# Turning a Gram product round and respacing a kernel's start: XCiT attention before a GELU feed-forward part

## The chip, the cores and the metric

The kernel runs on one core of a Trainium2 chip. The metric is the time of one execution in device microseconds (us), as the median of several executions. Where a single number of a profile is quoted, it is from one profiled execution, whose span is about 1.8 us shorter than its time. Engine names in the profile: PE is TensorE's matmuls, PEld its weight loads, DVE is VectorE, ACT is ScalarE, POOL is GpSimd, SP is SyncE; a q behind a name is the issuing of DMAs on that engine.

## The reference, cut to what matters

```python
B, N, C, D = 4, 6080, 256, 2048
qn = q / (np.linalg.norm(q, axis=1, keepdims=True) + 1e-06)   # norms over the N rows
kn = k / (np.linalg.norm(k, axis=1, keepdims=True) + 1e-06)
s = kn.transpose(0, 2, 1) @ qn / tau          # 256 x 256 per batch, summed over N
a = softmax(s)                                # over the last axis (q's columns)
x = v @ a                                     # (B, N, 256)
y = gelu_tanh(x @ w_in) @ w_out               # the feed-forward part, D = 2048
```

The kernel folds `a @ w_in` into one matrix `aw` per batch, so the stream is `hp = vT' @ aw`, a gelu on ScalarE and `yp = g' @ w_out`, in 12 blocks of up to 512 rows per batch.

## The kernel before

Batch 0 cannot start until its whole q and k are there: ten chunks of 128-row slots are loaded, cast to bf16, squared and multiplied into the Gram matrix `G`. Idle matmuls, whose results nobody reads, stand between the chunks to keep TensorE busy and so its clock full.

```python
first_chunks = chunks_of([6, 6, 6, 6, 6, 6, 4, 3, 2, 2], 7)  # slots; the 64 remainder rows ride on chunk 7
TAIL, SHARED = 6, 8
fillers = [0, 0, 5, 5, 5, 5, 3, 2, 1, 0]      # idle matmuls ahead of each chunk, for the clock

def stage_chunk(n):                           # called four chunks ahead
    ...                                       # chunks 8 and 9 share the buffers of 6 and 7
    load_chunk((nc.sync, nc.scalar if n < 1 else nc.sync), st, 0, first_chunks[n])   # (queue of q, of k)

def gram(G, qk, s, rows, first, last):        # G[i, j]: i = k's columns on the partitions
    for ic in range(2):
        nc.tensor.matmul(G[:, ic, :], lhsT=qk[:rows, 1, s, ic * 128 : ic * 128 + 128],
                         rhs=qk[:rows, 0, s, :], ...)

def scaled(G, r):                             # row i of G times 1/|k_i|, a value per partition
    for ic in range(2):
        nc.vector.tensor_scalar(Gs[:, ic, :], G[:, ic, :], r[:, 2 + ic : 3 + ic], inv_tau, ...)

def turned(Gs):                               # four fp32 transposes: T[j, i]
    ...

for n, ch in enumerate(first_chunks):         # batch 0
    nc.vector.tensor_copy(qkb[...], st[...])                  # L242, cast
    nc.scalar.activation(sqb[...], st[...], AF.Square)        # L247 (last two chunks: half on VectorE)
    keep_clock(fillers[n])
    ...                                                       # gram per slot, column sums of squares
    stage_chunk(n + 4)
    if n == n_chunks - 4:                                     # the gate: GpSimd's queue waits for chunk 6
        nc.gpsimd.tensor_copy(gate[:, 0:1], st[0:1, 1, 0, 0:1])
...
# behind the gate, on GpSimd's queue: w_in in four quarters, v of block 1, w_out in two halves,
# the first q and k of batch 1, v of block 2
load_v(1)
for half in range(2):
    nc.gpsimd.dma_start(out=wout_bf[...], in_=wout_v[...])
load_qk(1, 0)
load_v(2)
...
eT[:, jc, :] = exp(T[:, jc, :] * r[:, jc])    # 1/|q_j| as ScalarE's scale per partition
# first block: two of the four column groups of aw are made before it, the others within it
for i in range(NP):
    ...                                       # hp (L536 before, L533 after), gelu
    more_aw(1)                                # one of the four products left
```

v of block 2 and later ones is turned by DMA transposes on the sync queue once it has landed (`vT`).

## Time and profile before

| | before |
|---|---|
| time, median of 4 runs | 758.17 us (757.68 to 758.28) |
| profiled span | 756.4 us |
| first `hp` matmul (the feed-forward stream begins) | 43.19 us |
| span less that: the stream | 713.21 us |
| last piece of batch 0's q and k landed | 35.34 us |
| clock at half | 29.7 to 33.1 us |
| last column sum ends / both exponentials end | 38.24 / 41.32 us |

How to read it: the stream is TensorE alone, with no gap worth naming, so its 713.2 us are a constant of the work. Everything above 713.2 is the start, and the place of the first `hp` matmul is the one number that tells what a change to the start was worth. The timeline puts this matmul at 43.19 and the chain at 43.35; I use the timeline.

### The profile page before, as it was taken

Reading aid. Unit: us, or ns where it says so; the run is one execution under the profiler, and the core shown is the slowest. Engines: PE = TensorE matmul, PEld = TensorE weight load, DVE = VectorE, ACT = ScalarE, POOL = GpSimd, SP = SyncE. Lnnn points to the kernel's source line nnn. Section 1 sums busy time; section 2 is a strip of 40 time slices with the busy share of each in tenths; the row PEclk is TensorE's granted clock in tenths of the full one; section 3 lists DMA queues with packets and bytes.
Section 4 is the critical chain, followed back from the end, with each engine's and each line's share of the span. In section 5 each row is a group of like instructions: output and inputs, shape, how many; then the busy total and the mean of one; then the engine's idle time right before and its main releaser. Section 6 shows DMA issues by size and latency. Waiting matters only on the chain.

```text
span 756.4 us, 12305 instructions
## 1 busy us (share of the span) xinstructions
PE 738.3 (98%) x5248; PEld 504.5 (67%) x5248; DVE 278.2 (37%) x484; ACT 419.8 (56%) x411; POOL 70.7 (9%) x127
## 2 busy tenths in 40 slices
PE   4899999999999999999999999999999999999997
PEld 3556666667666666666666666666767666666666
DVE  4644545454402555553421455454441011011011
ACT  5675555555465555555555555555546655555552
POOL 0321011001021011001031000100101000000000
PEclk9999999999999999999999999999999999999999
DMA  8999957225149778313549375621412633322111
GB/s 364 355 206 168 177 84 155 54 42 83 42 93 215 134 137 132 73 43 64 102 93 220 83 135 96 126 79 47 82 42 79 110 83 72 68 76 52 41 57 56
DMA packets 80599, 83.59 MB, mean 111 GB/s; under 512 B 55456, under 2 KB 60064, under 8 KB 80544
## 3 DMA queue, kind: packets, MB, share of 16 engines
q0 software_dynamic: 17648, 32.97, 26.5%
q1 hardware_dynamic: 62672, 48.98, 24.3%
q8 instruction: 41, 0.67, 0.4%
q10 hardware_dynamic: 224, 0.85, 0.3%
q14 instruction: 14, 0.11, 0.1%
HBM read 78.91 MB, written 24.90 MB: 137 GB/s over the span
## 4 chain that ended last, share of the span: by engine, by line
PE 95%; DMA 3%; ACT 1%; DVE 0%; SPq 0%; issue 0%; DVEq 0%; ACTq 0%
PE yp L463 44%; PE hp L536 43%; PE G L141 5%; DMA st<-in_k_dram 3%; PE ps L201 2%; PE cols L153 1%; ACT sqb L247 0%; PE idle L137 0%; PE T L179 0%; DVE qkb L242 0%; SPq L80 0%; ACT g L540 0%; PE ps L345 0%; PE vps L333 0%; DVE Gs L171 0%
## 5 line engine op out<-in xcount | busy, mean ns | idle before, releaser
L540 ACT ACTIVATE g<-hp 128x1024 bf16<-128x1024 f32 (+1 forms) x384 | 389.3, 1014 | 308.9 <-PE hp L536 308.9
L463 PE MATMUL yp<-wout_bf,g 128*128 128x256 bf16 x3040 | 393.3, 273 | 0.0
L536 PE MATMUL hp<-vT,aw 128*128 128x512 bf16 (+1 forms) x1536 | 390.5, 377 | 0.2 <-ACT g L540 0.2
L463 PEld LDWEIGHTS <-g 128*128 128x128 bf16 x3040 | 297.5, 98 | 112.9
L536 PEld LDWEIGHTS <-aw 128*128 128x128 bf16 x1536 | 150.0, 98 | 105.3 <-issue 1.1
L480 DVE COPY ysb<-yp 128x512 f32<-128x512 f32 (+1 forms) x95 | 64.9, 683 | 403.1 <-PE yp L463 395.1
L404 DVE TENSOR_TENSOR acc<-acc,sq 128x512 f32<-128x512 f32 (+1 forms) x141 | 97.6, 692 | 4.8
L141 PE MATMUL G<-qkb 128*128 128x256 bf16 (+1 forms) x384 | 70.7, 285 | 13.6 <-DVE qkb L242 13.6
L403 DVE TENSOR_TENSOR sq<-qkb 128x512 bf16<-128x512 bf16 (+1 forms) x141 | 58.9, 418 | 0.0
L141 PEld LDWEIGHTS <-qkb 128*128 128x128 bf16 (+1 forms) x384 | 38.2, 102 | 23.0 <-DVE qkb L242 15.6
L280 POOL DMA_DIRECT2D vb<-in_v_dram x47 | 25.5, 544 | 142.8 <-DMA vT<-vb 135.9
L210 DVE TENSOR_SCALAR aw<-ps,rsinv 128x512 bf16<-128x512 f32 x30 | 22.3, 750 | 25.6 <-PE ps L201 25.3
L80 POOL DMA_DIRECT2D qkb<-in_q_dram x24 | 13.0, 540 | 152.1 <-PE hp L536 83.0
L247 ACT ACTIVATE sqb<-st 128x3072 bf16<-128x3072 f32 (+3 forms) x9 | 20.4, 2286 | 11.2 <-DMA st<-in_k_dram 11.2
L242 DVE CAST qkb<-st 128x3072 bf16<-128x3072 f32 (+4 forms) x11 | 14.7, 1345 | 14.9 <-DMA st<-in_k_dram 14.9
L201 PE MATMUL ps<-win_bf,eT 128*128 128x512 bf16 x60 | 17.7, 379 | 0.0
L414 POOL TENSOR_TENSOR r<-r,half 128x4 f32<-128x4 f32 x3 | 3.1, 1041 | 141.5 <-DVE r L413 141.5
L80 POOL DMA_DIRECT2D qkb<-in_k_dram x24 | 13.1, 544 | 5.0 <-DMA qkb<-in_q_dram 2.2
L521 POOL COPY g<-gr 128x1024 bf16<-128x1024 bf16 x2 | 2.1, 1037 | 104.1 <-PE yp L463 104.1
L439 DVE RECIPROCAL den<-den 128x256 f32<-128x256 f32 x6 | 10.5, 1753 | 0.2
L549 POOL COPY gr<-g 128x1024 bf16<-128x1024 bf16 x2 | 2.1, 1034 | 87.6 <-ACT g L540 87.6
L137 PE MATMUL idle<-filler 128*128 128x512 bf16 x32 | 9.2, 408 | 0.0
(60 smaller groups left out, 81.0 us busy)
## 6 DMA issues: line engine op xcount, KB each, us to landing
out_dram<-ysb SPq DMA_DIRECT2D x44, 512.0 KB, 2.9
vb<-in_v_dram POOLq DMA_DIRECT2D x43, 256.0 KB, 8.5
qkb<-in_q_dram POOLq DMA_DIRECT2D x21, 384.0 KB, 6.2
qkb<-in_k_dram POOLq DMA_DIRECT2D x21, 384.0 KB, 8.3
st<-in_q_dram SPq DMA_DIRECT2D x6, 768.0 KB, 10.3
st<-in_k_dram SPq DMA_DIRECT2D x5, 768.0 KB, 11.8
vT<-vb SPq DMA_TRANSPOSE x184, 3.8
out_dram<-ysb SPq DMA_DIRECT2D x4, 384.0 KB, 4.2
```

The costliest lines, as they stand in the source:

```text
L80: engines[x].dma_start(out=dst[:, x, 0:size, :], in_=src[b, s0 * 128 : (s0 + size) * 128, :].rearrange("(p s) c -> p s c", s=size))
L141: nc.tensor.matmul(G[:, ic, :], lhsT=qk[:rows, 1, s, ic * 128 : ic * 128 + 128], rhs=qk[:rows, 0, s, :], start=first and ic == 0, stop=las ...
L201: nc.tensor.matmul(ps, lhsT=eT[:, jc, ic * 128 : ic * 128 + 128], rhs=win_bf[:, jc, fs * 512 : fs * 512 + 512], start=jc == 0, stop=jc == 1)
L210: nc.vector.tensor_scalar_mul(dst, ps, scale)
L247: nc.scalar.activation(sqb[:rows, :, lo:hi], st[:rows, :, lo:hi], AF.Square)
L280: nc.gpsimd.dma_start(out=t[:, 0:n, :], in_=v_rows[r0 : r0 + n * 128, :].rearrange("(p s) c -> p s c", s=n))
L403: nc.vector.tensor_mul(sq[:rows], flat, flat)
L404: nc.vector.tensor_add(acc[:rows], acc[:rows], sq[:rows])
L463: nc.tensor.matmul(yp[:rows, at, :], lhsT=g[:, fc, s * 128 : s * 128 + rows], rhs=wout_bf[:, fc, :], start=fc == 0, stop=fc == FC - 1)
L480: nc.vector.tensor_copy(ysb[:, s0 : s + 1, :], yp[:, 0 : s + 1 - s0, :])
L536: nc.tensor.matmul(hp[:, j, :cols], lhsT=aw[:, cc, fc * 128 : fc * 128 + 128], rhs=vT[:, cc, :cols], start=cc == 0, stop=cc == 1)
L540: nc.scalar.activation(g[:, 2 * i : 2 * i + 2, :cols], hp[:, :, :cols], AF.Gelu_apprx_tanh)
```

## The change

The intent is twofold. In the softmax, the Gram product is turned round, so that q's columns lie on the partitions from the start and the four fp32 transposes go; k's norms, which then belong along the columns, are spread over all partitions by two small fp32 products with the identity. In the start, idle matmuls, chunk sizes, the remainder rows, two loads and the gate for the weights are put elsewhere.

```diff
-    first_chunks = chunks_of([6, 6, 6, 6, 6, 6, 4, 3, 2, 2], 7)
+    first_chunks = chunks_of([6, 6, 5, 6, 6, 6, 4, 4, 2, 2], 2)
-    fillers = [0, 0, 5, 5, 5, 5, 3, 2, 1, 0]
+    fillers = [0, 0, 5, 5, 6, 7, 2, 1, 0, 0]
-            load_chunk((nc.sync, nc.scalar if n < 1 else nc.sync), st, 0, first_chunks[n])
+            load_chunk((nc.sync, nc.scalar if n < 1 or n >= SHARED else nc.sync), st, 0, first_chunks[n])
 ...                                          (gram: q and k change places)
+        nc.vector.tensor_copy(Gs[:, 0, :], G[:, 0, :])
+        before_norms()
         for ic in range(2):
-            nc.vector.tensor_scalar(Gs[:, ic, :], G[:, ic, :], r[:, 2 + ic : 3 + ic], inv_tau, ...)
+            nc.tensor.matmul(along[:, ic * 128 : ic * 128 + 128],
+                             lhsT=r[:, 2 + ic : 3 + ic].to_broadcast([128, 128]), rhs=ident, ...)
+        nc.vector.tensor_copy(Gs[:, 1, :], G[:, 1, :])
+        for jc in range(2):
+            nc.vector.scalar_tensor_tensor(out=Gs[:, jc, :], in0=Gs[:, jc, :], scalar=inv_tau,
+                                           in1=along, op0=ALU.mult, op1=ALU.mult)
-    def turned(Gs):                          (the four transposes)
 ...
-        if n == n_chunks - 4:
+        if n == n_chunks - 3:                 (the gate now waits for chunk 7)
 ...
-    keep_clock(5)
+    keep_clock(3)
 ...
-                more_aw(1)
+                more_aw({0: 1, 2: 1, 4: 2}.get(i, 0))
```

More of the change, by code (lines that the diff above doesn't have):

```diff
@@ L139, in gram @@
     def gram(G, qk, s, rows, first, last):
-        for ic in range(2):
+        for jc in range(2):
             nc.tensor.matmul(
-                G[:, ic, :],
-                lhsT=qk[:rows, 1, s, ic * 128 : ic * 128 + 128],
-                rhs=qk[:rows, 0, s, :],
-                start=first and ic == 0,
+                G[:, jc, :],
+                lhsT=qk[:rows, 0, s, jc * 128 : jc * 128 + 128],
+                rhs=qk[:rows, 1, s, :],
+                start=first and jc == 0,
                 stop=last,
@@ L165, in norms, with scaled @@
         nc.vector.reciprocal(root, root)
-    def scaled(G, r):
+    def scaled(G, r, cols, before_norms):
         Gs = smx.tile([128, 2, 256], FP32, tag="Gs", name="Gs")
+        along = cols[:, 256:512]
+        nc.vector.tensor_copy(Gs[:, 0, :], G[:, 0, :])
+        before_norms()
         for ic in range(2):
-            nc.vector.tensor_scalar(Gs[:, ic, :], G[:, ic, :], r[:, 2 + ic : 3 + ic], inv_tau,
-                                    op0=ALU.mult, op1=ALU.mult)
-        return Gs
-    def turned(Gs):
-        T = pA.tile([128, 2, 256], FP32, tag="a", name="T")
-        for jc in range(2):
-            for ic in range(2):
-                nc.tensor.matmul(T[:, jc, ic * 128 : ic * 128 + 128],
-                                 lhsT=Gs[:, ic, jc * 128 : jc * 128 + 128],
-                                 rhs=ident, is_transpose=True)
-        return T
+            nc.tensor.matmul(along[:, ic * 128 : ic * 128 + 128],
+                             lhsT=r[:, 2 + ic : 3 + ic].to_broadcast([128, 128]),
+                             rhs=ident, start=True, stop=True, skip_group_check=True)
+        nc.vector.tensor_copy(Gs[:, 1, :], G[:, 1, :])
+        for jc in range(2):
+            nc.vector.scalar_tensor_tensor(out=Gs[:, jc, :], in0=Gs[:, jc, :], scalar=inv_tau,
+                                           in1=along, op0=ALU.mult, op1=ALU.mult)
+        return Gs
     def row_sums(eT):
@@ L259 @@
         stage_chunk(n + 4)
-        if n == n_chunks - 4:
+        if n == n_chunks - 3:
             nc.gpsimd.tensor_copy(gate[:, 0:1], st[0:1, 1, 0, 0:1])
@@ L321 @@
     nc.scalar.activation(dummy, ones_f, AF.Exp)
-    norms(r)
-    Gs = scaled(G, r)
-    keep_clock(5)
-    T = turned(Gs)
+    keep_clock(3)
+    Gs = scaled(G, r, cols, lambda: norms(r))
     eT = smx.tile([128, 2, 256], BF16, tag="eT", name="eT")
     for jc in range(2):
-        nc.scalar.activation(eT[:, jc, :], T[:, jc, :], AF.Exp, scale=r[:, jc : jc + 1])
+        nc.scalar.activation(eT[:, jc, :], Gs[:, jc, :], AF.Exp, scale=r[:, jc : jc + 1])
     vT0 = vts.tile([128, 2, 512], BF16, tag="vT", name="vT")
@@ L420, in attention_steps @@
         nc.vector.tensor_scalar_mul(rh, r[:, 0:2], 0.5)
-        Gs = scaled(G, r)
         yield
+        Gs = scaled(G, r, cols, lambda: None)
         yield
-        T = turned(Gs)
         eT = smx.tile([128, 2, 256], BF16, tag="eT", name="eT")
@@ L427, in attention_steps @@
             for jc in range(2):
-                nc.scalar.activation(eT[:, jc, :], T[:, jc, :], AF.Exp, scale=r[:, jc : jc + 1])
+                nc.scalar.activation(eT[:, jc, :], Gs[:, jc, :], AF.Exp, scale=r[:, jc : jc + 1])
             yield
@@ L433, in attention_steps @@
             for jc in range(2):
-                nc.scalar.activation(th[:, jc, :], T[:, jc, :], AF.Tanh, scale=rh[:, jc : jc + 1])
+                nc.scalar.activation(th[:, jc, :], Gs[:, jc, :], AF.Tanh, scale=rh[:, jc : jc + 1])
             for jc in range(2):
```

## The prediction

> **What bounds the kernel now.** I read the page first: TensorE is busy 98% of the span, and the chain that ended last is 95% TensorE, 87% of it the two products of the feed-forward part (lines 463 and 536). Then the same chain cut to the first 60 us, because the only large part of it that is not TensorE, 3% of DMA, must lie there.
>
> ```profile
> PE 738.3 (98%) x5248; PEld 504.5 (67%) x5248; DVE 278.2 (37%) x484; ACT 419.8 (56%) x411; POOL 70.7 (9%) x127
> PE 95%; DMA 3%; ACT 1%; DVE 0%; SPq 0%; issue 0%; DVEq 0%; ACTq 0%
> ```
>
> ```profile
> 13.95 13.28 DMA st<-in_k_dram
> ...
> 27.32 1.77 DVE qkb L242
> ...
> 29.14 2.25 PE G L141 x12
> 31.39 0.30 PE cols L153 x12
> 31.68 1.30 PE idle L137 x3
> 32.99 0.99 PE G L141 x8
> ...
> 38.05 0.19 PE cols L153 x8
> ...
> 43.35 0.86 PE hp L536 x4
> ```
>
> The columns are start, length and what it was. From 43.35 us on, TensorE is the bound without a gap worth naming: 756.4 - 43.35 = 713 us that only fewer matmul columns could shorten. Before that stands a start of 43 us: loads of batch 0's q and k until about 27 us on the chain, then TensorE working off what has come, then the small softmax. So the change can act in two places: in the start, and three more times in the softmax of the batches that run inside the matmul stream.
>
> The start has a detail that the chain does not explain: the 12 Gram matmuls at 29.14 take 2.25 us where the timeline has 1.48 us for the 12 of the chunks before. The table of windows gives the reason (columns: length; PE, PEld, DVE, ACT, POOL busy; granted clock; DMA share; GB/s).
>
> ```profile
> 28.00:29.00 1.00, 0.00 (x0) 0.00 (x0) 1.00 (x2) 1.00 (x1) 0.00 (x0) 1.00 1.04 402
> 29.50:30.00 0.50, 0.50 (x6) 0.41 (x4) 0.50 (x2) 0.50 (x1) 0.15 (x2) 0.68 1.03 365
> 30.50:31.00 0.50, 0.50 (x5) 0.32 (x3) 0.50 (x1) 0.50 (x1) 0.50 (x1) 0.50 1.09 252
> 33.00:33.50 0.50, 0.50 (x6) 0.45 (x5) 0.50 (x2) 0.50 (x1) 0.50 (x1) 0.91 1.15 279
> ```
>
> TensorE stood idle for 2.3 us (26.84 to 29.14, waiting for chunk 5), then its clock was half from about 29.66 to 33.1. That is 3.4 us at half rate, 1.7 us of work lost. It shows at the end: the last chunk's cast ends at 36.15, but its Gram matmuls start at 37.45, since TensorE is 1.3 us behind.
>
> **What the Trainium skill says.** "TensorE: Matmul & The Clock Gate", Part 1, has the clock at half after an idle window of about 3.4 us and free-running windows of that length; its closing table asks for no idle gaps above some 3 us. The trace agrees on the length of the slow stretch (3.4 us), but a gap of 2.3 us was enough. "DMA: Bandwidth & Descriptors", Issuing engines are not separate DMA queues: all queues share the same 16 engines, and a second issuing engine only saves issue time. Here issue time counts: the sync queue issued k of chunk 8 only at 27.25, just when k of chunk 5 had landed, eight issues on the same queue earlier. The same page's Specifications give about 1 us to the first byte for transfers issued from GpSimd. The trace disagrees: w_in is issued from 29.97, its first packets move at 33.0, 3.0 us later. "VectorE: DVE Perf Modes", Why PSUM operands drop a tier: fp32 from PSUM goes at single rate. The trace has 476 ns for 128x256 from PSUM, so I take that for the new operations too.
>
> **The change, part by part.**
>
> Softmax inside the stream (batches 1 to 3). Removed: four fp32 transposes, TensorE 182.27 to 182.71, so 0.44 us per batch. Added: two fp32 products of 128 columns. The trace shows 24 matmuls for the 12 fp32 column sums of three batches (two instructions each), eight of them from 172.78 to 173.59, 0.10 us each. Four instructions of 0.10 to 0.11 us: about 0.43 us. The balance is nil. VectorE gets two copies (0.9 us) more per batch, but sits idle for 4.99 us just before line 480 at 182.47; ScalarE's tanh loses its wait of 0.29 us for T, which holds nothing up. The turned Gram has the same matmuls. Sum: 0, within 0.3 us either way for all three.
>
> Softmax of batch 0, which is on the path. Before: last column sum ends 38.24, both exponentials end 41.32: 3.08 us. After, by the same durations, with the end of the column sums as 0: first copy of G until 0.4, norms until 0.8, the two small products (four instructions, with the first weight load and the drain) until 1.55, the second copy beside them, two scale operations until 2.05 and 2.5, second exponential until 2.97. Gain: 0.1 us. What the transposes cost comes back as products, so the change in the headline is worth almost nothing here.
>
> Loads. The remainder rows (64 rows in 1 KB pieces) move from chunk 7 to chunk 2; k of chunks 8 and 9 goes out on ScalarE's queue, so it does not wait for chunks 5 and 6; and the gate that lets the weights load waits for chunk 7 instead of 6. By 28 us the trace has moved 10.58 MB. Batch 0's q and k are 12.45 MB, so 1.87 MB are left, with some v in between. At the 0.37 to 0.40 MB per us of those microseconds, undisturbed by weights, the last piece lands at about 33.4 us instead of 35.4. An estimate. Gain: 2.0 us.
>
> Idle matmuls. They go to 5, 6, 7 before chunks 3, 4 and 5, and 2, 1, 0, 0 after. Seven of 0.22 us cover 0.4 us more of the gap, and the moved remainder should shorten it. If the clock stays full, TensorE is not 1.3 us behind. The last column sums would then end 1.4 us after the last landing (cast 0.69, square 0.43, sums): 34.8 instead of 38.24. The exponentials would be done at 37.8, a gain of up to 3.5 us.
>
> Weights. This is what cuts the gain. In the trace the GpSimd queue's next issues wait for the four quarters of w_in, which shows when these landed:
>
> ```profile
> 38.12 0.53 POOL L80 DMA_DIRECT2D qkb<-in_k_dram  x1 [0.94 <-DMA win_bf<-in_moe_w_in_dram]
> 39.35 0.53 POOL L85 DMA_DIRECT2D qkb<-in_q_dram  x1 [0.69 <-DMA win_bf<-in_moe_w_in_dram]
> 40.63 0.52 POOL L85 DMA_DIRECT2D qkb<-in_k_dram  x1 [0.76 <-DMA win_bf<-in_moe_w_in_dram]
> 42.26 0.55 POOL L280 DMA_DIRECT2D vb<-in_v_dram  x1 [1.10 <-DMA win_bf<-in_moe_w_in_dram]
> ```
>
> So 38.1, 39.3, 40.6 and 42.2. The first product with w_in stands at 41.5 today and has 3 us of slack; after the change it wants to start at 37.9. Gate about 31.75 (chunk 7), first weight packets 3.1 us later at 34.9, and then, with q and k out of the way, 0.195 MB per us as between 37 and 39 us: the 0.67 MB that had gone when the first quarter landed take until 38.3, the second quarter 39.6, the others 40.9 and 42.5. The first block's matmuls stand behind both quarters in TensorE's order: 39.6 + 0.9 = 40.5 instead of 43.35. Gain for the whole kernel: 2.85 us. The new places of the last four products with w_in (after pairs 0, 2, 4, 4 instead of 0 to 3) make sense just then: they put off the late quarters. By themselves they add no work, and the block is as long as before, about 9.5 us.
>
> **Rivals.** First, the weights do not bind: the gate opens earlier than I think, or the software queue is quicker alone. Then the full 3.5 to 4 us come: about 754. For it speaks that the writer moved the gate; against it that only 0.2 us stand between my landing times and the need. Second, the clock drops in the new wait: between 36 and 40 us TensorE would have some 2.4 us of work, 1 us of it transposes, no idle matmuls to spare. A slow stretch of 3.4 us in the first block costs up to 1.7 us: 756.5 to 757. Third, the loads are hidden or shift nothing: if the remainder delays chunk 3 as it may have delayed chunk 5, the last landing stays near 35, only the clock gain of 1.3 us is left: about 757. Fourth, wout or the next q and k come too late now that the first block starts earlier: wout landed at 48.6, is wanted at about 50.5 instead of 53.3, so 2 us of slack remain. Unlikely.
>
> **Range and chances.** 758.1 - 2.85 is 755.25; the first rival is somewhat less likely than the second and third together, which would say later, while the writer presumably kept what measured well, which says earlier. I stay at 755.3, with 753.6 to 757.2 for eight in ten. Two per cent would be 15 us, a third of the whole start. Neither side can reach that, so within 2% is nearly certain.
>
> **What would show it.** Right: the first hp matmul near 40.5 us, the stream after it unchanged at 713 us; the clock full from 29 to 34 us; last st landing near 33.4; TensorE waiting for w_in just before the first two pairs of ps; the small products at about 0.43 us per batch. Wrong: a stream longer or shorter than 713 us by over 0.5 us (then the softmax estimate fails), a half clock anywhere after 10 us, or exponentials that end late because the loads did not come sooner.

## The result, and the profile after

| | before | after | predicted for after |
|---|---|---|---|
| median (range), 4 runs each | 758.17 (757.68 to 758.28) | 759.40 (758.65 to 760.62) | 755.3 (753.6 to 757.2) |
| profiled span | 756.4 | 757.8 | |
| first `hp` matmul | 43.19 | 44.59 | 40.5 |
| stream after it | 713.21 | 713.21 | 713 |
| k of chunk 7 landed | 32.22 (its remainder 32.90) | 34.07 | |
| last piece of q and k landed | 35.34 | 35.36 | 33.4 |
| last column sum ends | 38.24 | 39.54 | 34.8 |
| clock at half | 29.7 to 33.1 | 35.7 to 39.1 | never |

The ratio is 1.0019, with a 95% interval from 1.0002 to 1.0036: the same within 2%, and just slower.

The stream is unchanged to the hundredth (756.4 - 43.19 and 757.8 - 44.59 are both 713.21), so all of the 1.4 us that the profiled run lost lies ahead of 44.6 us. The last piece of q and k landed when it did before, and yet the Gram product ended 1.3 us later. The engine shares of the chain that ended last hardly say so; only its first 45 us do (start, length, what):

```profile
PE 94%; DMA 4%; issue 1%; DVE 0%; ACT 0%; SPq 0%; DVEq 0%; ACTq 0%
```

```profile
22.28 11.79 DMA st<-in_k_dram
...
34.16 1.24 DVE qkb L242
...
35.45 1.68 PE G L142 x8
...
38.60 0.78 PE G L142 x4
...
44.75 0.86 PE hp L533 x4
```

Before, the chain left the loads at 27.2 us, with chunk 5, and TensorE carried it from there on. After, it stays with the loads until 34.07: one transfer, issued at 22.28, took 11.79 us. It is chunk 7's k. Behind it the eight Gram matmuls of that chunk take 1.68 us; in the timeline of the same kernel the eight of chunk 6, at full clock, take 1.05.

VectorE's casts show how the last chunks came in, first before, then after (start, length, engine, line, what, and in brackets the idle time ahead and what ended it):

```profile
32.31 1.55 DVE L242 CAST qkb<-st 128x1536 bf16<-128x1536 f32 x2 [0.33 <-DMA st<-in_k_dram]
34.10 0.69 DVE L242 CAST qkb<-st 128x1024 bf16<-128x1024 f32 x1 [0.25 <-DMA st<-in_k_dram]
35.46 0.69 DVE L242 CAST qkb<-st 128x1024 bf16<-128x1024 f32 x1 [0.20 <-DMA st<-in_k_dram]
```

```profile
34.16 1.86 DVE L242 CAST qkb<-st 128x2048 bf16<-128x2048 f32 x2 [1.26 <-DMA st<-in_k_dram]
36.41 0.69 DVE L242 CAST qkb<-st 128x1024 bf16<-128x1024 f32 x1
```

Before, chunks 7, 8 and 9 arrive one after the other, and each is worked off when it comes. After, VectorE waits 1.26 us for chunk 7 (the first line holds the casts of chunks 7 and 8) and then waits for nothing any more: the rest of chunks 8 and 9 landed at 34.73 and 35.36, while it was still at work on what came before. VectorE's work on them ends at 37.65, 2.3 us after the last landing instead of the 1.1 us that one chunk takes. The last pieces to land, before (k of chunk 9, issued at 29.81) and after (q of chunk 9, issued at 27.66), in narrow windows of `--dma` (size, us from issue to landing):

```profile
st<-in_k_dram SPq DMA_DIRECT2D x1, 256.0 KB, 5.5
```

```profile
st<-in_q_dram SPq DMA_DIRECT2D x1, 256.0 KB, 7.7
```

The queues say why. First before, 31 to 32 us; then after, 31 to 32 us and ScalarE's queue at 26 to 27 us (queue, packets, MB, share of the 16 engines); then the issues on ScalarE's queue in the kernel after:

```profile
q1 hardware_dynamic: 210, 0.37, 100.5%
```

```profile
q1 hardware_dynamic: 122, 0.25, 66.0%
q10 hardware_dynamic: 64, 0.13, 34.5%
```

```profile
q10 hardware_dynamic: 62, 0.13, 33.1%
```

```profile
22.39 0.34 ACTq L80 DMA_DIRECT2D st<-in_k_dram  x1
...
27.77 0.34 ACTq L80 DMA_DIRECT2D st<-in_k_dram  x1
```

q1 is the sync queue, q10 ScalarE's. k of chunk 8, issued at 22.39 right beside chunk 7's at 22.28, takes a third of the engines from 26 us on and has landed at 29.35, before chunk 7's own q (32.15). k of chunk 9, issued at 27.77, does the same from 31 us on. Both times chunk 7 still waits for its own. The bytes are no more than before and the engines are as full; they are served in another order.

The packed trace shows one thing more. Each transfer leaves sixteen landing marks, as many as there are engines, and its reader starts after the last. Up to q of chunk 5 the last follows the fifteenth within 0.1 us. From k of chunk 5 on it comes 1.3 to 2.2 us later for q and k on the sync queue, in both kernels: chunk 7's k has fifteen marks at 31.87 and the last at 34.07 (before, 30.62 and 32.22), the last piece 33.88 and 35.36 (before, 33.99 and 35.34). Run e11 shows where this begins.

The clock follows. TensorE has run out at 34.06, waits 1.39 us for chunk 7 with a single idle matmul ahead of the wait, and goes to half speed. Two windows of the kernel after (start:end, length; PE, PEld, DVE, ACT, POOL busy; granted clock; DMA share; GB/s):

```profile
34.00:35.00 1.00, 0.06 (x1) 0.00 (x0) 0.84 (x1) 0.82 (x1) 0.88 (x2) 1.00 0.47 184
36.50:37.00 0.50, 0.50 (x5) 0.38 (x4) 0.50 (x1) 0.50 (x2) 0.50 (x1) 0.50 0.82 115
```

In the first TensorE is busy for 0.06 us of one; in the second it is busy throughout, at a clock of 0.50.

The softmax inside the stream is what it was, in place and length. Before, then after:

```profile
182.27 0.60 PE L179 MATMUL T<-ident,Gs 128*128 128x128 f32 x4
```

```profile
181.96 0.61 PE L175 MATMUL cols<-ident,r 128*128 128x128 f32 x4
```

Four transposes out, four instructions of the two small products in; the matmuls that follow begin 0.44 us after the first of them before (182.71) and 0.45 us after (182.41).

Last, the gate that holds back the weights, before and after:

```profile
29.84 0.18 POOL L261 COPY gate<-st 1x1 f32<-1x1 f32 x1 [27.72 <-DMA st<-in_k_dram]
```

```profile
34.12 0.18 POOL L261 COPY gate<-st 1x1 f32<-1x1 f32 x1 [32.00 <-DMA st<-in_k_dram]
```

It opens 4.28 us later, since it now waits for the late chunk 7. Yet no product in this run waits for w_in. One caution: this trace has 5161 matmul records to 5246 weight loads, so some 85 are missing, and its busy sums are not compared with those of before.

### The profile page after: what moved, and what is told of

Its sections match the earlier page's. It is cut to its first block, busy times and chain, and to the rows that moved or that the text cites. A ratio compares the mean times of both kernels' runs of the same rounds, so it can differ in the third digit from the quotient of the medians.

```text
span 757.8 us, 12222 instructions
## 1 busy us (share of the span) xinstructions
PE 732.2 (97%) x5161; PEld 503.3 (66%) x5246; DVE 279.8 (37%) x492; ACT 419.3 (55%) x411; POOL 70.0 (9%) x127
## 3 DMA queue, kind: packets, MB, share of 16 engines
q10 hardware_dynamic: 512, 1.38, 0.5%
## 4 chain that ended last, share of the span: by engine, by line
PE 94%; DMA 4%; issue 1%; DVE 0%; ACT 0%; SPq 0%; DVEq 0%; ACTq 0%
PE yp L460 44%; PE hp L533 42%; PE G L142 5%; DMA st<-in_k_dram 4%; PE ps L201 2%; PE cols L154 0%; ACT g L537 0%; PE cols L175 0%; PE vps L373 0%; DVE qkb L242 0%; ACT eT L326 0%; PE ps L343 0%; SPq L80 0%; DVE r L165 0%; PE rs L188 0%
## 5 line engine op out<-in xcount | busy, mean ns | idle before, releaser
L533 PE MATMUL hp<-vT,aw 128*128 128x512 bf16 (+1 forms) x1458 | 384.6, 377 | 4.1 <-ACT g L537 0.2
```

Source lines behind the costliest of these rows:

```text
L533: nc.tensor.matmul(hp[:, j, :cols], lhsT=aw[:, cc, fc * 128 : fc * 128 + 128], rhs=vT[:, cc, :cols], start=cc == 0, stop=cc == 1)
```

## The experiments

Fourteen kernels ran, all with correct results. All had five rounds (e10 six runs), the one with fewer idle matmuls three (four runs). The intervals are about 1 us either way, so less than that is read from medians and ranges only. "Before" is the kernel before on the same chip. "First hp" is of the profiled run.

| run | median (range) | before | ratio [95%] | first hp |
|---|---|---|---|---|
| e1: softmax only | 757.94 (757.69 to 758.04) | 758.11 | 0.9999 [0.9987, 1.0012] | 42.98 |
| e2: all but the softmax | 759.73 (758.73 to 760.36) | 758.11 | 1.0022 [1.0009, 1.0034] | 44.08 |
| e3: after, late k on sync | 757.87 (757.29 to 758.63) | 758.11 | 0.9997 [0.9983, 1.0011] | 42.69 |
| e4: after, 8 idle matmuls | 759.36 (759.04 to 759.81) | 758.11 | 1.0019 [1.0007, 1.0032] | 44.21 |
| e5: after, gate back | 758.18 (757.99 to 759.05) | 758.05 | 1.0002 [0.9989, 1.0016] | 44.03 |
| e6: e3 and gate back | 757.02 (756.89 to 757.43) | 758.05 | 0.9986 [0.9973, 0.9999] | 41.82 |
| e7: before, idle moved | 757.99 (757.14 to 759.13) | 758.05 | 0.9999 [0.9986, 1.0011] | 43.15 |
| e8: e3, block 2's v early | 756.89 (756.61 to 757.71) | 758.05 | 0.9986 [0.9973, 0.9998] | 41.72 |
| e9: after, block 2's v early | 759.12 (758.59 to 759.62) | 758.18 | 1.0013 [1.0, 1.0025] | 42.82 |
| e10: e9, 5 idle matmuls | 759.03 (758.32 to 764.67) | 758.18 | 1.0009 [0.9996, 1.0023] | 43.77 |
| e11: e8, fewer idle matmuls | 758.47 (757.6 to 758.82) | 758.18 | 1.0003 [0.999, 1.0017] | 43.50 |
| e12: e6, block 2's v early | 756.93 (756.79 to 757.82) | 758.18 | 0.9987 [0.9975, 1.0] | 41.76 |
| e13: e5, 5 idle matmuls | 758.11 (758.08 to 758.33) | 758.14 | 1.0001 [0.9987, 1.0014] | 43.27 |
| e14: e6, chunks as before | 757.76 (757.53 to 758.33) | 758.14 | 0.9996 [0.9984, 1.0009] | 42.52 |

The theory after reading the two profiles: k on ScalarE's queue pushes chunk 7 back, and that costs the time. The rivals: the half clock costs it, the softmax costs it, or the later gate does.

**e1, the turned softmax alone.** Everything else of the change undone.

```diff
 # from the kernel after
-first_chunks = chunks_of([6, 6, 5, 6, 6, 6, 4, 4, 2, 2], 2)
+first_chunks = chunks_of([6, 6, 6, 6, 6, 6, 4, 3, 2, 2], 7)
 ...                 (idle matmuls, queue, gate and places of ps as before too)
```

> The kernel before with the turned Gram product alone (and the three idle matmuls in place of five ahead of it). Theory A (the start lost it, the softmax is neutral): within 0.5 us of before, column sums to second exponential about 3.1 to 3.2 us, first hp matmul at 43.2 to 43.6 us, stream of 713 us unchanged. Rival (the products or copies of the new softmax cost it): about 1.2 us slower than before.

757.94 beside 758.11: nothing, within the interval. The softmax of batch 0 took 2.86 us from the last column sum (38.26) to the end of the exponentials (41.12), 0.22 less than before.

**e2, all but the softmax.**

```diff
 # from the kernel before: chunks, idle matmuls, queue, gate and places of ps of the kernel after
```

> The kernel before with all changes of the start (chunks, idle matmuls, queue, gate, places of the late weight products) but the old softmax. Theory A: as slow as the changed kernel, 759.0 to 759.6 us, chunk 7 landing near 34.1 us and the clock at half for some 3.4 us from about 36 us. Rival: as before, 758.2 us.

759.73: the whole loss is here. So the part in the headline of the change is neutral in both directions of the test, within the intervals, and the respacing decides.

**e3, k of chunks 8 and 9 back on the sync queue.** One word of the change undone.

```diff
-load_chunk((nc.sync, nc.scalar if n < 1 or n >= SHARED else nc.sync), st, 0, first_chunks[n])
+load_chunk((nc.sync, nc.scalar if n < 1 else nc.sync), st, 0, first_chunks[n])
```

> The changed kernel with k of the last two chunks back on the sync queue. Theory O (these two transfers, on a queue of their own, take turns with chunk 7 and push it back by their 0.52 MB, 1.3 us at 0.41 MB per us): chunk 7 lands near 32.8 us, chunks 8 and 9 about 33.6 and 34.6, no half clock before the softmax, first hp matmul 42.2 to 43.0 instead of 44.75, total 756.8 to 757.8 us. Rival (one late DMA engine decides, whatever the queue): chunk 7 still near 34.1, total 759.4.

757.87, 1.53 less than the kernel after and just above the range expected. The cast of chunk 7 in e3:

```profile
33.31 2.04 DVE L242 CAST qkb<-st 128x2048 bf16<-128x2048 f32 x2 [0.52 <-DMA st<-in_k_dram]
```

It starts 10.43 us after that of chunk 4 (22.88), in the kernel after 11.81 (34.16 and 22.35): 1.38 us sooner. A count from the queues fits: k of chunk 8 is 0.26 MB and that of chunk 9 as much; 0.52 MB at the 0.41 MB that the kernel after moves in the microsecond before, 30 to 31, are 1.3 us. This is the queue theory's number. The marks split it in two: against chunk 4's cast, chunk 7's fifteenth mark comes 0.68 us sooner than in the kernel after (31.72 and 31.87), its last 1.38 (33.22 and 34.07). So the late last mark, the rival's one late engine, is there with either queue, and the queue comes on top. The last piece landed at 35.86, later than in the kernel after, and still the first `hp` matmul came sooner: it is not the last landing that counts. But this matmul moved by 1.90 us and the time by 1.5 only, and the profile holds a new wait, in block 2. The chain of e3, cut to its first 70 us, runs through it:

```profile
33.28 0.17 POOL gate L261
...
36.20 8.17 DMA win_bf<-in_moe_w_in_dram
...
44.66 11.01 DMA vb<-in_v_dram
...
60.37 7.49 DMA vT<-vb
...
68.10 1.02 PE hp L533 x4
```

Read from above: the gate opens at 33.28; w_in goes out; v of block 2 is the eighth issue behind w_in's last quarter on the same queue and is issued when that has landed, 44.66; it lands 11 us later, is turned by DMA transposes, and TensorE, which waits 0.74 us for it, goes on at 68.10. So a gate at 33 us reaches a matmul at 68. The profiled run was the slowest of its five, so the usual wait may be shorter.

**e4, eight idle matmuls before chunk 7.** If the half clock cost the time, this should bring it back.

```diff
-fillers = [0, 0, 5, 5, 6, 7, 2, 1, 0, 0]
+fillers = [0, 0, 5, 5, 6, 7, 2, 8, 0, 0]
```

> The changed kernel with eight idle matmuls instead of one ahead of chunk 7's Gram, to bridge the 1.4 us in which TensorE waits for it. Theory C (the half clock after that wait is part of the loss): clock full from 30 to 40 us, column sums end near 38.0 instead of 39.5, first hp matmul near 43.3, total 757.7 to 758.3 us. If the clock is not part of it: 759.4 us, or more if the idle matmuls themselves stand in the way.

759.36, as the kernel after (759.40). In the profiled run (clock 0.998 over the whole run) the half clock only came earlier, from 31.4 to 34.8, and the eight idle matmuls ran to 36.95 although chunk 7's data was ready at 35.9. The other four runs had a mean clock of 1.0. A slow stretch of 3.4 us would leave 0.998 (half of 3.4 is 0.2% of 757), so they had none, and still took 759.04 to 759.81. So with these idle matmuls in place a full clock does not bring the time back. That the half clock costs the kernel after nothing is not shown: its one run at a clock of 0.999 was its fastest (758.65, the others 759.17 to 760.62 at 0.996 or 0.997), and so was e2's one at 1.0 (758.73, the others 759.09 to 760.36).

**e5, the gate back on chunk 6; e6, gate and queue back.** With the kernel after and e3 they make a square of two by two.

```diff
 # e5 from the kernel after; e6 from e3
-        if n == n_chunks - 3:
+        if n == n_chunks - 4:
```

> The changed kernel with the gate of the weight loads back on chunk 6. Theory O (the order of the last loads is what lost time; weights were never waited for in the changed kernel): no gain, chunk 7 still lands at 34.0 to 34.6 us, first hp matmul 44.4 to 45.0, total 759.0 to 760.0 us. Rival G (the later gate lost the time): 758.2 us.

> The changed kernel with k of the last two chunks back on sync and the gate back on chunk 6. Theory V (with k on sync the rest of the gain went into a wait of block 2 for its transposed v, whose load stands behind the gated weights): the wait of 0.7 us at 68 us is gone, first hp matmul 42.7 to 43.3, stream back at 713.2 us, total 756.4 to 757.5 us. Rival (the weights now slow the last chunks): first hp matmul later than 43.3, total 757.9 or more.

| median, and in brackets less its own before | gate on chunk 7 | gate on chunk 6 |
|---|---|---|
| k of chunks 8, 9 on ScalarE's queue | 759.40 (+1.23) | 758.18 (+0.13) |
| on the sync queue | 757.87 (-0.24) | 757.02 (-1.03) |

e5 went against its expectation of no gain: 758.18 is the number of its rival, the gate. The queue costs 1.2 to 1.5 us in either column, with ranges that do not overlap; the gate 0.8 to 1.1 us in either row, with ranges that do; and the rest of the change gains 1.0 us. In the upper row a part of the gate's step may be the half clock: taking runs at a clock of 0.999 or more alone, it is 758.65 (one run) against 758.0 to 758.2. e6 is a version that beats both kernels. The square adds up within its spread: -1.03 + 1.16 + 0.79 makes +0.92, measured +1.23.

**e7, the kernel before with two idle matmuls more.** Do the moved idle matmuls alone give the gain?

```diff
 # from the kernel before
-fillers = [0, 0, 5, 5, 5, 5, 3, 2, 1, 0]
+fillers = [0, 0, 5, 5, 6, 7, 3, 2, 1, 0]
```

> The kernel before with the idle matmuls ahead of chunks 4 and 5 raised from 5 and 5 to 6 and 7, nothing else. Theory C (the half clock from 29.7 to 33.1 us puts TensorE 1.3 us behind at the end of the loads): clock full throughout, column sums end near 37.0 instead of 38.2, first hp matmul near 42.0, total 756.7 to 757.4 us. If TensorE's lag is hidden behind something else: 758.1 us.

A miss: 757.99, nothing gained. The clock was full from 28 to 40 us in the profiled run, but the cast of the last chunk only began at 36.15, so that the column sums ended at 38.18, as before (38.22 in the same view). e1, which has the loads of before too, also begins that cast at 36.14, and before's own profile at 35.46. So in these two profiles TensorE's lag of 1.3 us, which I had counted as lost, was hidden behind the last chunk, which landed at 36.0 us there and at 35.34 in before's own. Which of these is usual is not shown.

**e8, v of block 2 in front of w_out.** If the gate acts through block 2's v, as e3's chain says, an earlier load should give back the gate's cost with the gate left on chunk 7.

```diff
 # from e3
     load_v(1)
+    load_v(2)
     for half in range(2):
         nc.gpsimd.dma_start(out=wout_bf[...], in_=wout_v[...])
     load_qk(1, 0)
-    load_v(2)
```

> The changed kernel with k of the last two chunks on sync, gate still on chunk 7, and the load of block 2's v moved ahead of w_out and of the next q and k. Theory V: transposed v for block 2 is ready before 67 us, no wait at 68 us, first hp matmul near 42.7, total 756.4 to 757.2 us. If the wait is only replaced by one for w_out or for the next q and k: 757.5 us or more, with the wait at 53 to 57 us.

756.89, 0.98 less than e3 and as good as e6. Block 2's matmuls start without a wait, at the place where e3 had its wait. First e3, then e8:

```profile
68.10 1.02 PE L533 MATMUL hp<-vT,aw 128*128 128x512 bf16 x4 [0.74 <-DMA vT<-vb]
```

```profile
66.22 1.03 PE L533 MATMUL hp<-vT,aw 128*128 128x512 bf16 x3
```

So on the sync queue the gate's cost ran through block 2's v, all of it as far as the medians tell. A second version that beats both.

**e9, the same in the kernel after; e10, that with five idle matmuls before chunk 7.**

```diff
 # e9 from the kernel after: load_v(2) moved as in e8
 # e10 from e9
-fillers = [0, 0, 5, 5, 6, 7, 2, 1, 0, 0]
+fillers = [0, 0, 5, 5, 6, 7, 2, 5, 0, 0]
```

> The changed kernel with block 2's v loaded ahead of w_out and the next q and k; queue and gate as in the changed kernel. Theory two walls (late chunk 7 with the half clock holds back the first hp matmul; the late v of block 2 would hold back block 2 at about 68.5 us anyway): runs with a full clock fall from 758.7 to 757.8 to 758.3 us, runs with a half clock stay near 759, so a median of 758.0 to 759.0. If v is no wall in the changed kernel: 759.4 us as before.

> The same with five idle matmuls ahead of chunk 7 instead of one. Two walls: with the v wall gone, the bridge that gained nothing in the earlier run now pays: granted clock 0.999 or more in nearly all runs, first hp matmul 43.3 to 43.8 us, total 757.6 to 758.3 us. If the clock costs nothing here: the same as e9_after_v2_early within 0.3 us.

759.12 and 759.03, hardly less than 759.40: two misses, as 758.0 to 759.0 and 757.6 to 758.3 were expected. In e9 the first `hp` matmul stands 1.77 us sooner than in the kernel after, yet the stream lost 0.6 us of that to a wait for another transposed v, at 98.94 us. e10's profiled run was an outlier of 764.67, with waits for w_in (0.7), w_out (0.2) and block 2's v (3.31); its other runs had a clock of 0.999 to 1.0 and still took 758.3 to 759.3. So on ScalarE's queue the gate's cost does not run through block 2's v alone. Which wait carries it in a usual run is not shown: the profile of the kernel after has none for v there, and its block 2 starts at 69.09.

**e11, no idle matmuls before chunks 2 to 4.** This tests a side question. In all kernels so far chunk 5 came over 5 us after chunk 4, where chunks 3 and 4 are 3.8 apart. A packet of the instruction queue, at 24 to 25 us, lies in that gap. If the fetch comes with TensorE's instruction count, fewer idle matmuls should move it, and the gap with it.

```diff
 # from e8
-fillers = [0, 0, 5, 5, 6, 7, 2, 1, 0, 0]
+fillers = [0, 0, 0, 0, 0, 7, 2, 1, 0, 0]
```

> The kernel of e8_v2_early without the idle matmuls ahead of chunks 2, 3 and 4. Theory F (chunk 5 lands late because an instruction fetch of about 1.1 us on one DMA engine, triggered by TensorE's progress near 24.7 us, sets that engine back): with 16 pairs of instructions fewer the fetch comes after 27 us and chunk 5 lands at 25.9 to 26.6 us instead of 27.4. If the late landing has another cause: 27.4 us again. The total is not what this run is for (the clock will be half for longer).

The casts of chunk 5 in e8, then of chunks 5 and 6 in e11, and the instruction queue in e8 (24 to 25 us) and in e11 (28 to 29 us):

```profile
27.41 1.76 DVE L242 CAST qkb<-st 128x3072 bf16<-128x3072 f32 x1 [2.60 <-DMA st<-in_k_dram]
```

```profile
26.81 1.76 DVE L242 CAST qkb<-st 128x3072 bf16<-128x3072 f32 x1 [1.16 <-DMA st<-in_k_dram]
30.81 1.23 DVE L242 CAST qkb<-st 128x2048 bf16<-128x2048 f32 x1 [1.37 <-DMA st<-in_k_dram]
```

```profile
q8 instruction: 1, 0.02, 6.7%
```

```profile
q8 instruction: 1, 0.02, 6.8%
```

With chunk 4's cast at 22.18 in e8 and 23.03 in e11, chunk 5 came 5.23 us after it in e8 and 3.78 in e11; chunk 6 then came 2.57 us after chunk 5 in e8 and 4.00 in e11. The delay of 1.4 us moved from chunk 5 to chunk 6 together with the fetch. 6.7% of 16 engines for 1 us is 1.1 us of a single engine. The marks agree: chunk 5's k has its last two at 25.84 and 27.32 in e8 and at 26.70 and 26.72 in e11, where the lag begins with chunk 6's k (29.28 and 30.72). It then stays to the end of batch 0's loads (34.53 and 35.97): every landing after the fetch carries it, not one chunk alone. The landing itself, 26.81, is later than expected since the whole run was 0.85 us late at chunk 4. The time, 758.47, is 1.6 us above e8: leaving the idle matmuls out costs, though the runs do not tell how much of this is clock and how much arrival.

**e12, all three: queue and gate back, v of block 2 early.**

```diff
 # from e6: load_v(2) moved as in e8
```

> The changed kernel with k of the last two chunks on sync, the gate on chunk 6 and block 2's v early. Two walls: each of e6 and e8 alone already removed both, so nothing adds: 756.5 to 757.2 us, first hp matmul 41.5 to 42.2, no wait in the stream. If v or the weights still held something back there: below 756.4.

756.93, as e6 and e8: the gate back and v early repair the same wait, so nothing adds.

**e13, e5 with five idle matmuls before chunk 7.** e5's five runs fell in two groups, 758.0 to 758.2 at a clock of 0.999 to 1.0, and 759.0 twice at 0.997. If the half clock makes the second group, a bridge over the wait should end it.

```diff
 # from e5
-fillers = [0, 0, 5, 5, 6, 7, 2, 1, 0, 0]
+fillers = [0, 0, 5, 5, 6, 7, 2, 5, 0, 0]
```

> The changed kernel with the gate back on chunk 6 and five idle matmuls ahead of chunk 7 instead of one (k of the last chunks still on ScalarE's queue). If the half clock costs time where no v is late: the runs of e5_gate_back near 759.0 with a granted clock of 0.997 are gone, all runs at 0.999 or more and 757.7 to 758.2 us. If it does not: the same spread as e5_gate_back, 758.0 to 759.0.

758.08 to 758.33, all five at 0.999 or more; the slow pair is gone. The window of 36 to 37 us in the profiled runs of e5 and e13:

```profile
36.00:37.00 1.00, 1.00 (x8) 0.68 (x6) 1.00 (x2) 0.88 (x2) 1.00 (x2) 0.50 1.07 131
```

```profile
36.00:37.00 1.00, 1.00 (x24) 0.93 (x23) 0.97 (x3) 1.00 (x3) 1.00 (x2) 1.00 1.11 109
```

8 matmuls in that microsecond at a clock of 0.50, 24 at 1.00. So with the gate back the half clock costs 0.9 us in the runs that it hits (759.0 against 758.1; two runs of five, so how often is open). The median moves by 0.07 only, because most of e5's runs were not hit. With the gate on chunk 7 (e4, e10) a bridge buys nothing.

**e14, e6 with before's chunk sizes and the remainder on chunk 7.** What is e6's gain of 1.0 made of?

```diff
 # from e6
-first_chunks = chunks_of([6, 6, 5, 6, 6, 6, 4, 4, 2, 2], 2)
+first_chunks = chunks_of([6, 6, 6, 6, 6, 6, 4, 3, 2, 2], 7)
```

> e6_sync_gate_back with the chunk sizes of the kernel before and the remainder rows back on chunk 7. If the moved remainder gives the gain of that version (its last chunk then lands near 35.3 instead of 36.1 us): 757.8 to 758.2 us, as the kernel before. If the idle matmuls or the places of the late weight products give it: 757.0 us still.

757.76 beside e6's 757.02, and the ranges do not overlap: the moved remainder and the new sizes give about 0.7 of the 1.0 us. In the profiles the last cast starts at 35.65 instead of 35.27. Softmax, idle matmuls and the places of `ps` are left with 0.4 us, which the interval does not tell from nothing.

## Why the prediction was wrong, point by point

The prediction, 755.3 us, expected a gain of 2.85 us; the change lost 1.2. Its range ended at 757.2; that "within 2%" was nearly certain held.

**The softmax inside the stream: right.** It said 0.44 out and about 0.43 in per batch; measured 0.44 and 0.45. The stream kept its 713.21 us.

**The softmax of batch 0: right in size.** It said 2.97 instead of 3.08; e1 measured 2.86. In the kernel after itself it took 3.19, with one VectorE operation on the norms at 0.49 instead of 0.18 us. Neither decided anything.

**The loads: this step failed, and it is where the prediction broke.** It said "the last piece lands at about 33.4 us", and from there "The last column sums would then end 1.4 us after the last landing". The last piece landed at 35.36 us, where it had landed before (35.34): the gain of 2.0 us did not come. The sum had shared the bytes that were left among all sixteen engines at their mean rate. Fifteen of the last piece's sixteen marks do stand at 33.88, not far from the forecast; the last mark, which alone lets the work begin, lags 1.5 us. The second assumption that failed is that only the last chunk is still to be worked off then. It had quoted that all queues share the 16 engines, and took the second queue as saved issue time without asking from whom the earlier bytes are taken. They were taken from chunk 7, which was there at 34.07 instead of 32.90. The sum of the miss, 39.54 - 34.8 = 4.7 us, is made of three terms, rounded: 2.0 of later landing; 1.2 because VectorE, held up by chunk 7, ended 2.3 us after it (37.65) instead of 1.1; and 1.6 because TensorE ended 1.9 us after VectorE instead of 0.3, at half clock. Its own sign of being wrong, "exponentials that end late because the loads did not come sooner", came true: 42.7 us instead of 41.32.

**The idle matmuls: failed.** "If the clock stays full" did not hold: one idle matmul was left ahead of chunk 7, the wait there was 1.39 us, and the clock was half from 35.7 to 39.1. The clock did stay full over the wait for chunk 5, as the step said, although TensorE still stood idle for 2.08 us there (27.47 to 29.55). But that was worth nothing on its own: e7 took the half clock away, for which the prediction counted 1.3 us, and the time stayed.

**"The moved remainder should shorten" the wait for chunk 5: wrong cause.** That wait belongs to an instruction fetch (e11), and chunk 5 still came 5.38 us after chunk 4 (5.16 before). The moved remainder was worth about 0.7 us all the same, at the end of the loads (e14).

**The weights: wrong place.** It called them "what cuts the gain", with the gate at about 31.75. The gate opened at 34.12, and still the first block waited for no w_in, as everything else was later too. The later gate did cost 0.8 to 1.1 us. On the sync queue this ran through block 2's v (e3, e8): the fourth rival, called "Unlikely", and checked for w_out and the next q and k, but not for v.

**The rivals.** The second, a drop of the clock in the new wait, came true in kind, with 0.9 us in the runs it hits. The third, a last landing that "stays near 35", came true in number (35.36), though not for the reason it gave: chunk 3's cast starts at 18.57, at 18.37 before. No rival had two loads changing places, and none let the time go above 757, so the range was too low as well as too narrow.

So the change in sum: the softmax about nothing, the moved remainder and the rest -1.0, k on ScalarE's queue +1.2 to +1.5, the gate +0.8 to +1.1. What stays open is which wait carries the gate's cost when k is on ScalarE's queue, and how much of it is the half clock.

## What to carry to other kernels

Ask of a moved load not when the last byte lands, but when the piece lands that the consumer needs next: here a transfer on a second queue took its turns from the one in front of it. And count a landing at its last mark, not from the bytes at the mean rate of all engines: the fifteenth and the last were 1.5 us apart. A gain at the start of a kernel reaches only as far as the next loads allow, so look at the first two or three consumers behind it, transposes included, before a gate is put later. Test the parts of a change singly: here the part that gave it its name was neutral, two small ones cost 2 us together, and undoing them made a version that beat the kernel before by 1.0 us and the one after by 2.4.

## What the Trainium skill lacked or had wrong

- "TensorE: Matmul & The Clock Gate", Part 1 and the closing table: the advice to avoid idle gaps above some 3 us was too lax here. Gaps of 2.3 us (before) and 1.39 us (after) were followed by a stretch of 3.4 us at half clock; one of 2.08 us (after, chunk 5) was not. With five idle matmuls ahead of the wait for chunk 7 the clock stayed at 1.00 (e13). So no single length of gap decides; the page's free-running windows agree with that: in the traces' clock records the slow stretches last 3.41 us, and the recorded stretches of full clock just ahead of them 13.65 (before) and 23.89 us (after), 4 and 7 times as long.
- "DMA: Bandwidth & Descriptors", Issuing engines are not separate DMA queues: it says that starting DMAs on several engines only saves issue time. Here it also changed the order of arrival: 0.25 MB for the sync queue and 0.13 MB for ScalarE's in the same microsecond, chunk 7 1.38 us later, and 1.2 to 1.5 us of the kernel's time. The same page's Queues, rings and completion order has each engine go round the queue rows that have work, which agrees; the consequence for a load that is waited for is not drawn.
- The same page, Specifications: about 1 us to the first byte for transfers issued from GpSimd. w_in's first packets came 3.0 us after the issue before (29.97 to 33.0), and about 1.8 to 2.0 us after it in the kernel after (34.25, first packets between 36.0 and 36.25).
- "Runtime: NRT & Kernel Launch", Instruction fetch mechanics: it calls the cost of a fetch mostly hidden. TensorE did not wait for it, but the fetch held one of the 16 DMA engines for 1.1 us (6.7% of 16 engines in 1 us), and a load in flight landed 1.4 us later; with 16 idle matmuls fewer the delay moved from chunk 5 to chunk 6 (e11), and all later landings of batch 0 carried it.
